# Moving the decay factors of a retention layer to k and to the evacuation, with fronts scheduled further ahead of the channel mixer

## The chip, the cores and the metric

The kernel runs on one core of one Trainium2 chip. The metric is device time in microseconds (us). Times are medians of all executions. Two executions fell into a slower state that has a longer span; the ratios leave them out. A ratio is the mean time of one kernel's fast runs over the mean of the other's fast runs of the same rounds, so it isn't quite the ratio of the medians that stand beside it.

## The reference

Four batches, eight heads, 768 steps, head size 64. First a linear attention with decay, then a mixer over tokens and one over channels (d_tok 256, d_ch 1536):

```python
state = gamma * state + einsum('bhd,bhe->bhde', k[:, :, t], v[:, :, t])
y[:, :, t] = scale * einsum('bhd,bhde->bhe', q[:, :, t], state)
x  = y of all heads side by side                  # [batch, 768, 512]
u  = x + (relu(x^T @ w_tok1) @ w_tok2)^T          # token mixer
out = u + relu(u @ w_ch1) @ w_ch2                 # channel mixer
```

## The kernel before

The recurrence runs in six chunks of 128 steps. The decay inside a chunk is split into two factors that depend on the position alone: one on q, one on v. A **front** is the work on one pair of heads of one batch, attention and token mixer, up to `uT`, the transposed input of the channel mixer; four fronts make a batch. The channel mixer is the **back**. As to the engines: DVE scales q, POOL casts k and scales v, PE does products and transposes, ACT evacuates.

```python
def front(b, p):                                   # eleven steps, a yield after each
    kc = nc.gpsimd.tensor_copy(k16, kf)            # L138 (access patterns cut)
    for j in range(2):                             # one head each
        nc.gpsimd.tensor_scalar(v16[:, :, j, :], vf[...], gv[:, h:h + 1], None, ALU.mult)   # L142
    for j in range(2):
        nc.vector.tensor_scalar(q16[:, :, j, :], qf[...], gq[:, h:h + 1], None, ALU.mult)   # L146
    yield kc
    ...                        # k transposed; k^T v into U (DVE), q transposed, masks (DVE, L192)
    nc.scalar.copy(xo, y)                          # L207, y leaves PSUM
    nc.gpsimd.tensor_copy(x16, xo)                 # L208, f16 for the token mixer
    ...                        # L214, relu, L224 token mixer; L227 add on DVE; L228 cast of u on POOL
    nc.scalar.copy(uT[:, p], tp)                   # L233

for p in range(NP):
    load(0, p)                                     # k, v, q of a pair: three DMAs on one queue (q1)
for s, p, kc in fronts(0):
    if s == 0 and p in (0, 3):
        with tc.issue_after(kc.ins):               # POOL issues the weights (q0) when it gets there
            load_weights(p // 3)
for b in range(B):
    if b + 1 < B:
        ...                                        # loads of b + 1; steps of its fronts
    for us in back(b):                             # spread between the steps of the mixer of b
        ...
```

Every engine works through its own instructions in the order that the build gives it, so an instruction that waits holds all that stand behind it.

## Time and profile before

| | before |
|---|---|
| time, median (lowest to highest) | 251.18 us (250.8 to 251.71) |
| span of the profiled run, granted clock | 249.1 us, 0.984 |
| last uT copy of batch 0 ends | 57.3 us |
| PE idle from there to 245.4 | 13.7 us |
| busy PE / DVE / ACT / POOL | 208.8 / 116.8 / 106.4 / 92.3 us |

```profile
kf<-in_k_dram SPq DMA_DIRECT2D x1, 384.0 KB, 9.0
```

One of six weight transfers goes out at 29.8, and the other five only after 36.9: in between, POOL waits 2.77 us for an add of DVE, casts u (1.13) and scales v (2.46). This k, issued at 29.41, lands 9.0 us later, at 38.4, when the five have hardly begun: from 36 to 40 the weights' queue moves 0.07 MB.

### The profile page before, as it was taken

What the parts mean: (1) busy time and instruction counts of PE and PEld (TensorE: products, weight loads), DVE (VectorE), ACT (ScalarE), POOL (GpSimd) and SP (SyncE); (2) the same over time, 40 slices, a digit from 0 to 9 for tenths busy, and PEclk for the clock granted to TensorE, in tenths of its full rate; (3) what the DMA queues carried; (4) which work ended last, traced back from release to release, by engine and by line L of the source; (5) the groups of instructions that cost most, each with busy time, mean ns of one, the idle gap of its engine ahead of it and who ended that gap; (6) DMA issues with size and microseconds to landing.
All of it is one profiled execution on the core that took longest, in us unless ns stands there. A gap on an engine that the chain in (4) does not pass through costs nothing.

```text
span 249.1 us, 4702 instructions
## 1 busy us (share of the span) xinstructions
PE 208.8 (84%) x1888; PEld 133.6 (54%) x1888; DVE 116.8 (47%) x270; ACT 106.4 (43%) x211; POOL 92.3 (37%) x128
## 2 busy tenths in 40 slices
PE   1448675679989797889798898799899999999994
PEld 0347564456646574456555564466556665554641
DVE  3466447915747445327566445136455354203012
ACT  2233443208804582228615480248435743450710
POOL 4654669943543433621616253520511203100000
PEclk9999999959999999999999999999999999999999
DMA  8999999999949992949862001110011002102112
GB/s 160 228 232 221 204 213 190 196 196 235 214 102 234 228 220 39 216 105 233 153 163 89 0 3 42 42 45 0 3 64 66 0 3 86 45 0 84 42 45 84
DMA packets 82198, 29.41 MB, mean 118 GB/s; under 512 B 75008, under 2 KB 79104, under 8 KB 82176
## 3 DMA queue, kind: packets, MB, share of 16 engines
q1 hardware_dynamic: 77952, 25.17, 49.1%
q0 software_dynamic: 4224, 3.93, 9.6%
q8 instruction: 15, 0.25, 0.4%
q14 instruction: 7, 0.06, 0.1%
HBM read 26.74 MB, written 6.29 MB: 133 GB/s over the span
## 4 chain that ended last, share of the span: by engine, by line
PE 59%; POOL 22%; ACT 7%; DMA 3%; issue 3%; DVE 2%; SPq 2%; POOLq 0%; DVEq 0%; ACTq 0%
PE acc L261 21%; PE acc L253 19%; POOL v L142 14%; PE acc L214 4%; POOL x L208 3%; PE acc L224 3%; DMA vf<-in_v_dram 3%; PE acc L189 3%; ACT h L256 3%; PE tp L232 2%; POOL u L228 2%; SPq L121 2%; PE tp L155 2%; POOL k L138 2%; ACT qT L157 1%
## 5 line engine op out<-in xcount | busy, mean ns | idle before, releaser
L253 PE MATMUL acc<-uT,wc 128*128 128x384 f16 x384 | 74.5, 329 | 0.0
L261 PE MATMUL acc<-wc,h 128*128 128x512 f16 x288 | 71.7, 379 | 0.0
L256 ACT ACTIVATE h<-acc 128x384 f16<-128x384 f32 x96 | 46.7, 498 | 25.0 <-PE acc L253 24.0
L192 DVE TENSOR_TENSOR am<-acc,mask 128x384 f16<-128x384 f32 x64 | 32.8, 551 | 34.4 <-PE acc L189 34.3
L253 PEld LDWEIGHTS <-wc 128*128 128x128 f16 x384 | 34.5, 99 | 18.3 <-issue 0.5
L142 POOL TENSOR_SCALAR v<-vf,gv 128x384 f16<-128x384 f32 x32 | 40.2, 1265 | 8.8 <-DMA vf<-in_v_dram 6.7
L261 PEld LDWEIGHTS <-h 128*128 128x128 f16 x288 | 25.5, 98 | 21.8
L228 POOL CAST u<-x 128x384 f16<-128x384 f32 x32 | 15.8, 510 | 53.0 <-DVE x L227 52.7
L208 POOL CAST x<-x 128x384 f16<-128x384 f32 x32 | 16.5, 518 | 49.3 <-ACT x L207 45.4
L214 PE MATMUL acc<-x,wt 128*128 128x128 f16 x192 | 18.3, 239 | 18.2 <-POOL x L208 18.0
L266 DVE TENSOR_TENSOR o<-x,acc 128x512 f32<-128x512 f32 x24 | 16.5, 686 | 33.5 <-PE acc L261 33.2
L233 ACT COPY uT<-tp 128x768 f16<-128x768 f16 x16 | 12.8, 797 | 41.2 <-PE tp L232 41.2
L214 PEld LDWEIGHTS <-wt 128*128 128x128 f16 x192 | 14.6, 107 | 23.1 <-issue 20.6
L207 ACT COPY x<-acc 128x384 f32<-128x384 f32 x32 | 15.5, 484 | 22.6 <-PE acc L204 22.2
L227 DVE TENSOR_TENSOR x<-x,acc 128x384 f32<-128x384 f32 x32 | 16.6, 550 | 15.9 <-PE acc L224 15.2
L175 DVE SCALAR_TENSOR_TENSOR U<-U,gp,acc 128x128 f32<-128x128 f32 x64 | 22.1, 346 | 2.6
L173 DVE COPY U<-acc 128x128 f32<-128x128 f32 x16 | 4.7, 292 | 35.6 <-PE acc L167 35.6
L146 DVE TENSOR_SCALAR q<-qf,gq 128x384 f16<-128x384 f32 x32 | 18.5, 602 | 5.5 <-DMA qf<-in_q_dram 5.4
L204 PE MATMUL acc<-v,am 128*128 128x64 f16 x192 | 16.7, 205 | 0.7 <-DVE am L192 0.7
L204 PEld LDWEIGHTS <-am 128*128 128x128 f16 x192 | 14.4, 106 | 4.8 <-DVE am L192 0.9
L216 ACT ACTIVATE h<-acc 128x256 f16<-128x256 f32 x16 | 6.1, 380 | 25.4 <-PE acc L214 25.3
L157 ACT COPY qT<-tp 128x768 f16<-128x768 f16 x16 | 12.7, 794 | 9.5 <-PE tp L155 9.5
(40 smaller groups left out, 192.7 us busy)
## 6 DMA issues: line engine op xcount, KB each, us to landing
kf<-in_k_dram SPq DMA_DIRECT2D x16, 384.0 KB, 6.5
vf<-in_v_dram SPq DMA_DIRECT2D x16, 384.0 KB, 6.3
qf<-in_q_dram SPq DMA_DIRECT2D x16, 384.0 KB, 6.5
out_dram<-o SPq DMA_DIRECT2D x24, 256.0 KB, 2.0
wc<-in_moe_w_ch_dram POOLq DMA_DIRECT2D x6, 512.0 KB, 11.4
wt<-in_moe_w_tok_dram POOLq DMA_DIRECT2D x2, 384.0 KB, 7.0
```

The costliest lines, as they stand in the source:

```text
L142: nc.gpsimd.tensor_scalar(v16[:, :, j, :], vf[:, j * NC:(j + 1) * NC, :], gv[:, h:h + 1], None, ALU.mult)
L146: nc.vector.tensor_scalar(q16[:, :, j, :], qf[:, j * NC:(j + 1) * NC, :], gq[:, h:h + 1], None, ALU.mult)
L175: nc.vector.scalar_tensor_tensor(U[:, c], U[:, c - 1], gp[:, p:p + 1], s, ALU.mult, ALU.add)
L192: nc.vector.tensor_tensor(am, a[j][:, :HC], mask, ALU.mult)
L204: nc.tensor.matmul(o[:, j * D:(j + 1) * D], ams[2 * hf + j][:, i], v16[:, c, j], start=(c == 0), stop=(c == 0 or j == 1))
L208: nc.gpsimd.tensor_copy(x16[:, hf * HC:(hf + 1) * HC], xo)
L214: nc.tensor.matmul(acc[:, jt * P:(jt + 1) * P], wt1[:, i, jt * P:(jt + 1) * P], x16[:, i], start=(i == 0), stop=(i == NC - 1))
L227: nc.vector.tensor_tensor(xo, xo, acc[:, :HC * P].rearrange("p (i d) -> p i d", d=P), ALU.add)
L228: nc.gpsimd.tensor_copy(u16[:, hf * HC:(hf + 1) * HC], xo)
L253: nc.tensor.matmul(acc[:, :SH], w[:, ct, (ft % FW) * P:(ft % FW + 1) * P], uT[:, ct, sh * SH:(sh + 1) * SH], start=(ct == 0), stop=(ct == ...
L256: nc.scalar.activation(h2[:, ft], acc[:, :SH], AF.Relu)
L261: nc.tensor.matmul(acc, h2[:, ft, i * P:(i + 1) * P], wc2[ft // FW][:, ft % FW], start=(ft == 0), stop=(ft == NF - 1))
```

## The change

The factors move. One factor now sits on k alone (`gk`), which must be multiplied anyway, and the factor that was on q is applied to the finished y as it leaves PSUM. So q and v need only casts. The schedule is rebuilt too: steps of fronts and mixer are put in a list ordered by an assumed time, with the fronts up to two batches ahead, and the loads of batch 1 are asked for within the fronts of batch 0. The token weights go out with pair 1 in place of pair 0. Buffer counts are cut or raised to fit.

```diff
-        kc = nc.gpsimd.tensor_copy(k16..., kf...)
-            nc.gpsimd.tensor_scalar(v16..., vf..., gv[:, h:h + 1], None, ALU.mult)   # two heads
-            nc.vector.tensor_scalar(q16..., qf..., gq[:, h:h + 1], None, ALU.mult)   # two heads
+            nc.vector.tensor_scalar(k16..., kf..., gk[:, h:h + 1], None, ALU.mult)   # two heads
+        vc = nc.gpsimd.tensor_copy(v16..., vf...)
+        nc.gpsimd.tensor_copy(q16..., qf...)                    # a step later
...
-            nc.scalar.copy(xo, y...)
+            if hf == 0:                                         # ACT, one head at a time
+                nc.scalar.mul(x[...], yv[...], gy[:, h:h + 1])
+            else:                                               # DVE, gyw = gy made wide at setup
+                nc.vector.tensor_tensor(x[...], yv, g.to_broadcast([P, HC, P]), ALU.mult)
...
+        if s == 3:
+            load(1, p, after=ins if p < 3 else None)            # ins: the copy of qT, pair p of batch 0
...
+            f0 = t0 + 10.0 if b == 0 else t0 - LEAD             # LEAD 9, mixer 31, front 16 model units
+            f1 = t0 + PERIOD - LEAD
+            add(fronts(b + 1, 5), [f0 + (f1 - f0) * i / n for i in range(n)], ("front", b + 1))
```

The argument `after` makes a load of batch 1 wait for ACT's copy of qT of the same pair of batch 0, for the first three pairs.

More of the change, by code (lines that the diff above doesn't have):

```diff
@@ L48 @@
     am_p = ctx.enter_context(tc.tile_pool(name="amp", bufs=8))
-    x_p = ctx.enter_context(tc.tile_pool(name="xp", bufs=2))
+    x_p = ctx.enter_context(tc.tile_pool(name="xp", bufs=3))
     mlp_p = ctx.enter_context(tc.tile_pool(name="mlp", bufs=2))
@@ L70 @@
     nc.vector.tensor_scalar(lgs, lgs, itp, None, ALU.mult)
-    gq = const_p.tile([P, H], FP, name="gq")
-    gv = const_p.tile([P, H], FP, name="gv")
-    nc.scalar.activation(gv, lgs, AF.Exp, scale=-1.0)
-    nc.scalar.activation(gq, lgs, AF.Exp, bias=lnsc, scale=1.0)
+    gk = const_p.tile([P, H], FP, name="gk")
+    gy = const_p.tile([P, H], FP, name="gy")
+    nc.scalar.activation(gk, lgs, AF.Exp, scale=-1.0)
+    nc.scalar.activation(gy, lgs, AF.Exp, bias=lnsc, scale=1.0)
     ident16 = const_p.tile([P, P], F16, name="ident16")
@@ L87 @@
     )
+    gyw = const_p.tile([P, H, D], FP, name="gyw")
+    nc.vector.memset(gyw, 1.0)
+    for h in range(H):
+        nc.gpsimd.tensor_scalar(gyw[:, h], gyw[:, h], gy[:, h:h + 1], None, ALU.mult)
     NR = 3
@@ L115, with load @@
     loaded = {}
-    def load(b, p):
+    def load(b, p, after=None):
         got = []
@@ L120, in load @@
             t = load_p.tile([P, 2 * NC, D], FP, name=f"{nm}f")
-            nc.sync.dma_start(
+            dma = nc.sync.dma_start(
                 out=t, in_=src[b, 2 * p:2 * p + 2].rearrange("h (c p) d -> p (h c) d", p=P))
+            if after is not None:
+                tc.add_manual_dep(
+                    dma.ins, after.ins.name,
+                    mybir.DependencyInfo(mybir.DependencyClass.Sync, mybir.DependencyReason.DATA),
+                    reason="the weights come first")
             got.append(t)
@@ L134, in front, with half @@
         kf, vf, qf = loaded.pop((b, p))
-        q16 = att_p.tile([P, NC, 2, D], F16, name="q16")
-        k16 = att_p.tile([P, NC, 2, D], F16, name="k16")
-        v16 = att_p.tile([P, NC, 2, D], F16, name="v16")
-        kc = nc.gpsimd.tensor_copy(k16.rearrange("p c h d -> p h c d"),
-                                   kf.rearrange("p (h c) d -> p h c d", h=2))
+        def half(hf):
+            return slice(hf * HC, (hf + 1) * HC)
+        k16 = att_p.tile([P, NC, 2, D], F16, name="k16", bufs=2)
+        v16 = att_p.tile([P, NC, 2, D], F16, name="v16", bufs=3)
+        q16 = att_p.tile([P, NC, 2, D], F16, name="q16", bufs=2)
         for j in range(2):
             h = 2 * p + j
-            nc.gpsimd.tensor_scalar(v16[:, :, j, :], vf[:, j * NC:(j + 1) * NC, :],
-                                    gv[:, h:h + 1], None, ALU.mult)
-        for j in range(2):
-            h = 2 * p + j
-            nc.vector.tensor_scalar(q16[:, :, j, :], qf[:, j * NC:(j + 1) * NC, :],
-                                    gq[:, h:h + 1], None, ALU.mult)
-        yield kc
-        qT = att_p.tile([P, S], F16, name="qT")
-        kT = att_p.tile([P, S], F16, name="kT")
+            nc.vector.tensor_scalar(k16[:, :, j, :], kf[:, j * NC:(j + 1) * NC, :],
+                                    gk[:, h:h + 1], None, ALU.mult)
+        vc = nc.gpsimd.tensor_copy(v16.rearrange("p c h d -> p h c d"),
+                                   vf.rearrange("p (h c) d -> p h c d", h=2))
+        yield vc
+        qT = att_p.tile([P, S], F16, name="qT", bufs=3)
+        kT = att_p.tile([P, S], F16, name="kT", bufs=3)
         def turn(src, dst):
@@ L156, in turn @@
                                     src[:, c].rearrange("p h d -> p (h d)"), ident16)
-            nc.scalar.copy(dst, tp[:, :S])
+            return nc.scalar.copy(dst, tp[:, :S])
         turn(k16, kT)
+        nc.gpsimd.tensor_copy(q16.rearrange("p c h d -> p h c d"),
+                              qf.rearrange("p (h c) d -> p h c d", h=2))
         yield
-        U = att_p.tile([P, NC - 1, P], FP, name="U")
+        U = att_p.tile([P, NC - 1, P], FP, name="U", bufs=2)
         R = r16[(b * NP + p) % NR]
@@ L179, in front @@
         yield
-        turn(q16, qT)
-        yield
+        turned = turn(q16, qT)
+        yield turned
         ams = []
@@ L194, in front @@
             yield
-        x16 = att_p.tile([P, NC, P], F16, name="x16")
+        x16 = att_p.tile([P, NC, P], F16, name="x16", bufs=2)
         for hf in range(2):
@@ L205, in front @@
                                      start=(c == 0), stop=(c == 0 or j == 1))
-            xo = x[:, hf * HC:(hf + 1) * HC, pc]
-            nc.scalar.copy(xo, y[:, :HC * P].rearrange("p (i d) -> p i d", d=P))
-            nc.gpsimd.tensor_copy(x16[:, hf * HC:(hf + 1) * HC], xo)
+            yv = y[:, :HC * P].rearrange("p (i d) -> p i d", d=P)
+            if hf == 0:
+                for j in range(2):
+                    h = 2 * p + j
+                    nc.scalar.mul(x[:, half(hf), h * D:(h + 1) * D], yv[:, :, j * D:(j + 1) * D],
+                                  gy[:, h:h + 1])
+            else:
+                g = gyw[:, 2 * p:2 * p + 2].rearrange("p (o h) d -> p o (h d)", o=1)
+                nc.vector.tensor_tensor(x[:, half(hf), pc], yv, g.to_broadcast([P, HC, P]), ALU.mult)
+            nc.gpsimd.tensor_copy(x16[:, half(hf)], x[:, half(hf), pc])
             yield
-        h1 = att_p.tile([P, NJ, P], F16, name="h1")
+        h1 = att_p.tile([P, NJ, P], F16, name="h1", bufs=2)
         acc = bank()
@@ L217, in front @@
         yield
-        u16 = att_p.tile([P, NC, P], F16, name="u16")
+        u16 = att_p.tile([P, NC, P], F16, name="u16", bufs=2)
         for hf in range(2):
@@ L225, in front @@
                                      start=(jt == 0), stop=(jt == NJ - 1))
-            xo = x[:, hf * HC:(hf + 1) * HC, pc]
+            xo = x[:, half(hf), pc]
             nc.vector.tensor_tensor(xo, xo, acc[:, :HC * P].rearrange("p (i d) -> p i d", d=P), ALU.add)
-            nc.gpsimd.tensor_copy(u16[:, hf * HC:(hf + 1) * HC], xo)
+            nc.gpsimd.tensor_copy(u16[:, half(hf)], xo)
         yield
@@ L236, with fronts @@
     NS = 11
-    SKEW = 5
-    def fronts(b):
+    def fronts(b, skew):
         gens = [front(b, p) for p in range(NP)]
-        for _, s, p in sorted((SKEW * p + s, s, p) for p in range(NP) for s in range(NS)):
+        for _, s, p in sorted((skew * p + s, s, p) for p in range(NP) for s in range(NS)):
             yield s, p, next(gens[p])
+    BACK_STEPS = 2 * (NF * [0.65] + HC * 3 * [0.86])
     def back(b):
@@ L256, in back @@
                 nc.scalar.activation(h2[:, ft], acc[:, :SH], AF.Relu)
-                yield 0.65
+                yield
             for i in range(HC):
@@ L263, in back @@
                     if ft % 4 == 3 and ft < NF - 1:
-                        yield 0.86
+                        yield
                 o = o_p.tile([P, C], FP, name="o")
@@ L268, in back, with add @@
                 nc.sync.dma_start(out=out[b, t0:t0 + P, :], in_=o)
-                yield 0.86
+                yield
     for p in range(NP):
         load(0, p)
-    for s, p, kc in fronts(0):
-        if s == 0 and p in (0, 3):
-            with tc.issue_after(kc.ins):
+    for s, p, ins in fronts(0, 4):
+        if s == 0 and p in (1, 3):
+            with tc.issue_after(ins.ins):
                 load_weights(p // 3)
-    BACK_US = 31.0
-    for b in range(B):
-        steps = None
-        if b + 1 < B:
-            for p in range(NP):
-                load(b + 1, p)
-            steps = fronts(b + 1)
-        spent, done, total = 0.0, 0, NP * NS
-        for us in back(b):
-            spent += us
-            while steps and done < total and done < spent / BACK_US * total:
-                next(steps)
-                done += 1
-        for _ in steps or ():
-            pass
+        if s == 3:
+            load(1, p, after=ins if p < 3 else None)
+    FRONT_US, BACK_US, LEAD = 16.0, 31.0, 9.0
+    PERIOD = FRONT_US + BACK_US
+    todo = []
+    def add(steps, times, kind):
+        for n, t in enumerate(times):
+            todo.append((t, len(todo), steps, kind))
+    for b in range(B):
+        t0 = b * PERIOD
+        gen = back(b)
+        us = BACK_STEPS
+        span = PERIOD if b + 1 < B else BACK_US
+        run = 0.0
+        times = []
+        for d in us:
+            times.append(t0 + run / BACK_US * span)
+            run += d
+        add(gen, times, ("back", b))
+        if b + 1 < B:
+            f0 = t0 + 10.0 if b == 0 else t0 - LEAD
+            f1 = t0 + PERIOD - LEAD
+            n = NP * NS
+            add(fronts(b + 1, 5), [f0 + (f1 - f0) * i / n for i in range(n)], ("front", b + 1))
+    for t, _, gen, (kind, b) in sorted(todo, key=lambda e: e[:2]):
+        got = next(gen)
+        if kind == "front" and b + 1 < B and got[0] == 3:
+            load(b + 1, got[1])
 _INS = ['q', 'k', 'v', 'moe_w_tok1', 'moe_w_tok2', 'moe_w_ch1', 'moe_w_ch2']
```

## The prediction

> **What bounds the kernel now.** I read the page of the kernel before first: busy shares, the forty slices, the chain that ended last.
>
> ```profile
> PE 208.8 (84%) x1888; PEld 133.6 (54%) x1888; DVE 116.8 (47%) x270; ACT 106.4 (43%) x211; POOL 92.3 (37%) x128
> PE   1448675679989797889798898799899999999994
> DMA  8999999999949992949862001110011002102112
> PE 59%; POOL 22%; ACT 7%; DMA 3%; issue 3%; DVE 2%; SPq 2%; POOLq 0%; DVEq 0%; ACTq 0%
> ```
>
> One slice is 6.2 us. PE is below 8 in most of the first nine slices, mostly 8 or 9 in the middle and full to the end but for the last store, where only the channel mixer of the last batch runs. DMA is full for about 70 us and then nearly idle. POOL, busy for only 37%, carries 22% of the chain. So there are three stages with three limits.
>
> I then cut the span into those stages and took the busy time of each engine:
>
> ```profile
> 0.00:57.00 57.00, 34.11 (x318) 27.47 (x319) 30.62 (x82) 17.43 (x31) 36.27 (x51) 0.94 1.19 205
> 57.00:214.50 157.50, 143.78 (x1407) 90.07 (x1406) 82.08 (x182) 76.75 (x156) 56.00 (x77) 1.00 0.47 101
> 214.50:245.40 30.90, 30.90 (x167) 16.02 (x164) 3.43 (x5) 12.24 (x25) 0.00 (x0) 1.00 0.14 52
> ```
>
> The columns are the stretch, its length, then PE, PEld, DVE, ACT and POOL busy. I put the first cut at 57 because the chain in order of time shows the last uT copy of batch 0 at 56.51; only then can the mixer run unhindered. The middle has 157.5 - 143.8 = **13.7 us of PE idle**; the last stretch has none. After 245.4 there are 3.7 us of final add and store. The run time exceeds the span by about 2 us (251.3 against 249.1).
>
> Next, the groups by line and the waits of PE, to see who stops it:
>
> ```profile
> L142 POOL TENSOR_SCALAR v<-vf,gv 128x384 f16<-128x384 f32 x32 | 40.2, 1265 | 8.8 <-DMA vf<-in_v_dram 6.7
> L208 POOL CAST x<-x 128x384 f16<-128x384 f32 x32 | 16.5, 518 | 49.3 <-ACT x L207 45.4
> L146 DVE TENSOR_SCALAR q<-qf,gq 128x384 f16<-128x384 f32 x32 | 18.5, 602 | 5.5 <-DMA qf<-in_q_dram 5.4
> PE acc L214 <- POOL x L208: 12.8, 9, 1.8
> ```
>
> The last line is the wait list for 54 to 190: nine waits, 12.8 us in all, the longest 1.8. The token mixer's first matmuls (L214) wait for POOL's cast of x, and that explains nearly all of the 13.7 us. The POOL timeline says why the cast is late:
>
> ```profile
> 102.86 0.51 POOL L208 CAST x<-x 128x384 f16<-128x384 f32 x1 [1.98 <-ACT x L207]
> 103.52 2.46 POOL L142 TENSOR_SCALAR v<-vf,gv 128x384 f16<-128x384 f32 x2 [0.15 <-PE acc L204]
> 105.93 0.50 POOL L208 CAST x<-x 128x384 f16<-128x384 f32 x1
> ```
>
> Between the two halves of one pair's x, POOL scales the next pair's v for 2.46 us; L214 starts at 106.48 after an idle of 1.82.
>
> In the start the same instruction rules. The last q of batch 0 is issued at 21.31 and lands some 6.4 us later, at 28, yet the front ends at 57. From 40 to 54 POOL is busy 10.8 of 14 us: v scaling for batch 0 and already for batch 1, casts, and the descriptors of the channel weights.
>
> **What the Trainium skill says.** "GPSIMD Engine Reference", section 4.1, calls POOL about 2x slower than VectorE for two-input work and roughly line rate for one input. The trace agrees only for the cast: the k cast of 768 elements takes 844 ns, 1.1 ns each, while the per-partition scale takes 3.3 ns each (1265 over 384).
>
> "SBUF — State Buffer", "Who interferes with whom": VectorE and GpSimd share a port pair, taken for a whole instruction, and a VectorE tensor_scalar can take it. The trace fits: DVE's q scale takes 404 ns at its shortest and 2400 at its longest, beside POOL's v.
>
> "DMA: Bandwidth & Descriptors", "Queues, rings and completion order": an engine round-robins between queues by packet. From 40 to 44 us the trace agrees (packets, MB, share):
>
> ```profile
> q0 software_dynamic: 613, 0.61, 91.0%
> q1 hardware_dynamic: 616, 0.16, 29.3%
> ```
>
> With equal packet counts the weights move 0.153 MB/us and the loads 0.04, against about 0.22 alone.
>
> "ScalarE: Activation LUTs", "What ACT_TABLE_LOAD costs", gives 186 ns + 0.833 ns an element, and 93 more for a pointer operand. The 384-element copy fits: 506 against 484.
>
> **The change part by part**, per pair of heads (16 pairs).
>
> POOL loses the k cast (0.84) and two v scales (2.53), and gains casts of v and q (0.84 each). With the x and u casts, two halves each, it goes from 5.43 to 3.74 us a pair, 27 us in all. Setup adds eight small scales for gyw: 64 x 3.3 ns plus some 0.1, near 0.3 us each, 2.5 in all, before v lands.
>
> DVE trades the q scale for an equal k scale and gains one evacuation of y, about 0.55 (the mask product of the same shape and source takes 551 ns). That is +8.8 us in all, less any time no longer lost to POOL's lock. Per batch DVE needs about 32 us, in a PE period of about 47.
>
> ACT replaces two copies (0.97) by two scaled copies of 192 elements. The skill's formula gives 186 + 160 + 93 = 439 ns each, so 0.88: nothing to speak of.
>
> PE has the same instructions. From the stage table the steady work and the last mixer are 143.8 + 30.9 = 174.7 us of busy time; with what front 1 did before 57 I take **175.5**.
>
> *The steady stage.* POOL's block between two x casts shrinks from 2.46 to 0.83 (or two of 0.83), a gain of up to 1.63 where the waits were 1.1 to 1.8. So most of the 12.8 us should go. Fronts also run about 9 model units ahead of the mixer, so a late uT no longer stops the next batch. Against it: the second half of y now queues in DVE behind a chain of U updates (1.9 us). I leave **4.5 us** of stalls.
>
> *The start.* The loads follow each other every 1.75 us, the first landing at 4.66: the twelfth at 4.66 + 11 x 1.75 = 23.9. The token weights, 0.79 MB, hold the loads back for about 5 us at a fifth of their rate: 4.2 more, so the last q lands at 28, as now. From there one front needs the q cast 0.83, transposes 0.65, copy 0.8, products 0.5, mask 1.0, y 0.7, evacuation 0.55, x cast 0.5, the two token products 1.3 each, relu 0.4, add 0.55, cast 0.5, transposes 0.65 and copy 0.8. That is 11.0 us, with 2.5 of semaphore steps 13.5 us. POOL also issues six weight transfers at 0.79, right after the v cast of pair 3 and so ahead of its q cast: 4.7 us, most of which I count, 3.5. Front 0 ends at 28 + 13.5 + 3.5 = **45** in place of 57.
>
> Are the weights there? Issued near 28 to 33, 3.15 MB at 0.155 MB/us take 20 us: all landed by about 49. The first half is in by 39, and the second is needed some 10 us after 45. Good. The loads of batch 1 then have about 10 of 12 to go: 49 + 17.5 = 66. The dense fronts of batch 1 want their last pair near 70, the second already near 53: a wait of 1 or 2 us, inside my 4.5.
>
> Sum: 45 + 175.5 + 4.5 + 3.7 = 228.7 of span; with 2 us more about **230 us**, against 251.3.
>
> **The rivals.**
> (a) *The start is bound by DMA, not POOL.* Batches 0 and 1 and all weights are about 25 + 25 + 24 us of transfer, and they keep DMA full to 74 us either way. If the fronts of batch 1 are issued ahead of their loads, PE and DVE, which work in order, stand still on k. The trace has two such waits for v (6.7 us) already. Against it: the mixer of batch 0 offers 31 us of independent PE work. It would cost 5 to 8 us: about 237.
> (b) *The wait moves from POOL to DVE.* y's second half, k, U, mask and the add are then all on one queue, and L214 waits for DVE instead. DVE's 32 of 47 us speaks against a bound, its bursts speak for some waits. If half of the 13 us stay, 233 to 235.
> (c) *POOL's descriptor block in the start.* If it keeps pair 3 back as v does now, front 0 ends at 50: 235.
> (d) *Everything is hidden and PE is the floor.* Front 0 ends at 41, stalls of 1: 221.
> (e) No gain would need both the start and the waits to be rebuilt elsewhere; I see no term that large.
>
> **Range and chances.** The end of front 0 (41 to 51) and the stalls (1 to 9) are the two loose terms, and the rest is PE time that was measured. Together 220 to 240. Within 2% of before means over 246, which needs the start gain gone and half the waits kept: 6%. Slower: 1%.
>
> **What will show it.** PE busy unchanged, near 205 to 209. POOL down to about 65, DVE up to about 125. L214's wait for x near zero. The last uT copy of batch 0 near 45, and PE nearly solid from there. If I am wrong by more than the range, I expect PE waiting on the first transposes of batch 1 (rival a), or L214 waiting behind DVE (rival b). Two things could falsify the sum altogether: the order of the instructions, which the build chooses and I can't see, and a lower PE rate in the denser start: the twelve L224 matmuls took 1.44 us near 52 and 0.67 later.

## More of the kernel before

One more view matters for what came later: when POOL issued the channel weights (start, duration, instruction, count), and how long the second pair of batch 1 took to load when it was issued at 29.41.

```profile
29.80 0.82 POOL L106 DMA_DIRECT2D wc<-in_moe_w_ch_dram  x1
...
34.51 2.46 POOL L142 TENSOR_SCALAR v<-vf,gv 128x384 f16<-128x384 f32 x2
36.93 1.55 POOL L106 DMA_DIRECT2D wc<-in_moe_w_ch_dram  x2
38.46 2.36 POOL L110 DMA_DIRECT2D wc<-in_moe_w_ch_dram  x3
```

## The result, and the profile after

The changed kernel takes **247.87 us** (246.64 to 248.13) against 251.18: a ratio of 0.9855, 95% interval 0.9823 to 0.9888. It is 1.4% faster, within the 2% that I had called the same; I had predicted 8.5%, and the measured time lies outside my range of 220 to 240.

The page of the kernel after: busy time, PE and its granted clock in 40 slices of 6.1 us, and the chain that ended last by engine.

```profile
PE 203.7 (83%) x1888; PEld 129.3 (53%) x1888; DVE 119.8 (49%) x287; ACT 105.1 (43%) x211; POOL 68.7 (28%) x120
PE   0475745016998999999999999999999999999993
PEclk9999985555899999999999999999999999999998
PE 63%; DMA 17%; POOL 8%; issue 6%; ACT 3%; DVE 2%; SPq 0%; POOLq 0%; DVEq 0%; ACTq 0%
```

From the eleventh slice on PE is full: the middle did what I expected. But in the eighth and ninth, where before has 6 and 7, PE stands at 0 and 1, and DMA has gone from 3% to 17% of the chain. By stage (stretch, length, PE, PEld, DVE, ACT, POOL busy, granted clock, DMA share, GB/s):

```profile
40.00:60.00 20.00, 4.09 (x40) 3.34 (x39) 4.00 (x9) 1.31 (x3) 4.29 (x7) 0.50 1.21 210
...
80.00:210.10 130.10, 128.45 (x1276) 80.91 (x1274) 75.79 (x171) 66.34 (x136) 35.97 (x62) 1.00 0.42 95
210.10:241.30 31.20, 31.16 (x169) 16.25 (x166) 4.13 (x6) 11.77 (x24) 0.00 (x0) 1.00 0.14 51
```

Hardly an engine works from 40 to 60, only the DMA does; in the same stretch of the kernel before PE was busy for 15.23 us. The rows by line that answer to L142, L214 and L146 of before (busy, mean ns, idle ahead of them and what ended it) confirm the costs: the v cast takes 851 ns (the q cast 847), and the waits for x are down to 2.0 us at the token mixer (L233). What is new is the k scale's idle time.

```profile
L156 POOL CAST v<-vf 128x768 f16<-128x768 f32 x16 | 13.6, 851 | 15.8 <-DMA vf<-in_v_dram 13.3 <-PE acc L216 2.4
L233 PE MATMUL acc<-x,wt 128*128 128x128 f16 x192 | 16.6, 236 | 4.7 <-DMA wt<-in_moe_w_tok_dram 2.5 <-POOL x L227 2.0
L154 DVE TENSOR_SCALAR k<-kf,gk 128x384 f16<-128x384 f32 x32 | 14.5, 464 | 19.0 <-DMA kf<-in_k_dram 18.9
```

The timeline of DVE shows which k (in brackets the idle time ahead and what ended it):

```profile
35.48 1.39 DVE L154 TENSOR_SCALAR k<-kf,gk 128x384 f16<-128x384 f32 x2
53.10 0.75 DVE L154 TENSOR_SCALAR k<-kf,gk 128x384 f16<-128x384 f32 x2 [16.22 <-DMA kf<-in_k_dram]
53.76 1.94 DVE L204 TENSOR_TENSOR am<-acc,mask 128x384 f16<-128x384 f32 x4
55.62 1.01 DVE L246 TENSOR_TENSOR x<-x,acc 128x384 f32<-128x384 f32 x2
```

The k at 35.48 belongs to pair 0 of **batch 1**, the k at 53.10 to pair 1 of batch 1. Behind it in the same queue stand the masks (L204) of batch 0's last pair and the add (L246) of the pair ahead of it. From 45 to 66, PE's longest wait is put down to exactly those masks (L243 is the second product of the token mixer, here of the pair ahead):

```profile
PE acc L243 <- DVE am L204: 14.3, 1, 14.3
```

Everything of batch 0 stops: its last uT copy starts at 64.16 in place of 56.51. POOL is caught likewise, and the first two lines of its timeline say why the data were late:

```profile
28.55 2.31 POOL L111 DMA_DIRECT2D wc<-in_moe_w_ch_dram  x3
30.84 2.24 POOL L115 DMA_DIRECT2D wc<-in_moe_w_ch_dram  x3
...
44.20 0.83 POOL L170 CAST q<-qf 128x768 f16<-128x768 f32 x1 [7.53 <-DMA qf<-in_q_dram]
54.84 0.83 POOL L156 CAST v<-vf 128x768 f16<-128x768 f32 x1 [9.82 <-DMA vf<-in_v_dram]
```

POOL issues all six weight transfers in one block, by 33.1. (The lighter v isn't the only reason: `schedule_only` below keeps the v scaling and has them out by 34.8.) This k is issued at 30.05, hardly later than the 29.41 of before, but now the weights are in the DMA engines with it. The DMA view from 36 to 40 and the transfer itself (KB, us from issue to landing):

```profile
q0 software_dynamic: 612, 0.61, 89.7%
q1 hardware_dynamic: 611, 0.16, 29.3%
...
kf<-in_k_dram SPq DMA_DIRECT2D x1, 384.0 KB, 23.0
```

Packet for packet the queues are even, so in bytes the loads get 0.16 MB in 4 us, 0.04 MB/us. With the weights gone, from 52 to 56, they move 0.94 MB in 4 us. The k takes 23.0 us in place of 9.0: at 0.04 MB/us its own 384 KB and those still ahead of it need about that.

So the balance of spans is: the start is 7.7 us longer (65.0 against 57.3, each the end of that uT copy), what follows up to the last store is 11.8 shorter (176.3 against 188.1), the tail equal; together 4.1, and the spans differ by 4.2 (249.1 against 244.9; the profile of the changed kernel is of its fastest execution, and the medians differ by 3.3).

### The profile page after: what moved, and what is told of

The parts are those of the page before. It is cut to its first block, busy times and chain, and to the rows that moved or that the text cites. A ratio compares the mean times of both kernels' runs of the same rounds, so it can differ in the third digit from the quotient of the medians.

```text
span 244.9 us, 4710 instructions
## 1 busy us (share of the span) xinstructions
PE 203.7 (83%) x1888; PEld 129.3 (53%) x1888; DVE 119.8 (49%) x287; ACT 105.1 (43%) x211; POOL 68.7 (28%) x120
## 2 busy tenths in 40 slices
DMA packets 82198, 29.41 MB, mean 120 GB/s; under 512 B 75008, under 2 KB 79104, under 8 KB 82176
## 4 chain that ended last, share of the span: by engine, by line
PE 63%; DMA 17%; POOL 8%; issue 6%; ACT 3%; DVE 2%; SPq 0%; POOLq 0%; DVEq 0%; ACTq 0%
PE acc L281 22%; PE acc L273 21%; DMA qf<-in_q_dram 12%; PE acc L233 5%; PE acc L243 3%; DMA wt<-in_moe_w_tok_dram 3%; PE tp L165 3%; PE acc L201 3%; PE tp L251 3%; DMA vf<-in_v_dram 2%; POOL v L156 2%; POOL q L170 2%; POOL x L227 2%; POOL gyw L92 1%; POOL u L247 1%
## 5 line engine op out<-in xcount | busy, mean ns | idle before, releaser
L273 PE MATMUL acc<-uT,wc 128*128 128x384 f16 x384 | 72.8, 327 | 0.0
L204 DVE TENSOR_TENSOR am<-acc,mask 128x384 f16<-128x384 f32 x64 | 32.4, 552 | 14.6 <-PE acc L201 14.2
L286 DVE TENSOR_TENSOR o<-x,acc 128x512 f32<-128x512 f32 x24 | 16.5, 686 | 43.2 <-PE acc L281 42.9
L243 PE MATMUL acc<-h,wt 128*128 128x128 f16 x192 | 15.3, 236 | 15.0 <-DVE am L204 14.3
L154 DVE TENSOR_SCALAR k<-kf,gk 128x384 f16<-128x384 f32 x32 | 14.5, 464 | 19.0 <-DMA kf<-in_k_dram 18.9
L243 PEld LDWEIGHTS <-wt 128*128 128x128 f16 x192 | 13.5, 106 | 18.1 <-issue 15.9
L246 DVE TENSOR_TENSOR x<-x,acc 128x384 f32<-128x384 f32 x32 | 16.4, 550 | 13.1 <-PE acc L243 12.6
L222 ACT ACTIVATE x<-acc,gy 128x192 f32<-128x192 f32 x32 | 11.8, 429 | 21.8 <-PE acc L216 21.8
L233 PE MATMUL acc<-x,wt 128*128 128x128 f16 x192 | 16.6, 236 | 4.7 <-DMA wt<-in_moe_w_tok_dram 2.5
L170 POOL CAST q<-qf 128x768 f16<-128x768 f32 x16 | 13.6, 847 | 23.3 <-DMA qf<-in_q_dram 8.5
L233 PEld LDWEIGHTS <-wt 128*128 128x128 f16 x192 | 13.9, 106 | 8.9 <-issue 3.9
L156 POOL CAST v<-vf 128x768 f16<-128x768 f32 x16 | 13.6, 851 | 15.8 <-DMA vf<-in_v_dram 13.3
L167 ACT COPY kT<-tp 128x768 f16<-128x768 f16 x16 | 12.8, 802 | 11.7 <-PE tp L165 11.7
```

The costliest lines, as they stand in the source:

```text
L156: vc = nc.gpsimd.tensor_copy(v16.rearrange("p c h d -> p h c d"), vf.rearrange("p (h c) d -> p h c d", h=2))
L167: return nc.scalar.copy(dst, tp[:, :S])
L170: nc.gpsimd.tensor_copy(q16.rearrange("p c h d -> p h c d"), qf.rearrange("p (h c) d -> p h c d", h=2))
L204: nc.vector.tensor_tensor(am, a[j][:, :HC], mask, ALU.mult)
L233: nc.tensor.matmul(acc[:, jt * P:(jt + 1) * P], wt1[:, i, jt * P:(jt + 1) * P], x16[:, i], start=(i == 0), stop=(i == NC - 1))
L243: nc.tensor.matmul(acc[:, i * P:(i + 1) * P], wt2[:, jt, t], h1[:, jt], start=(jt == 0), stop=(jt == NJ - 1))
```

## The experiments

My theory after the comparison: **two in-order queues, DVE and POOL, carry conversions of batch 1 ahead of the last work of batch 0, and those conversions wait for loads that share the DMA engines with the weights.** Rivals: one queue alone is to blame; the loads are late for another reason (the explicit dependency); fronts start too early; or one half of the change, scaling or schedule, does the harm and the other the good. Fourteen kernels were run. The column "PE 40–80" is PE's busy time between 40 and 80 us, a measure of how open the start is.

| run | time, us | ratio to before | last uT copy of batch 0 starts | PE 40–80 |
|---|---|---|---|---|
| before | 251.18 | | 56.51 | 33.82 |
| after | 247.87 | 0.9855 | 64.16 | 22.60 |
| order_dve, order_pool (one run each) | 247.13, 247.45 | | 64.61, 64.60 | 22.46, 22.90 |
| order_both | 237.06 | 0.9431 | 47.72 | 33.44 |
| late_weights | 244.81 | 0.9743 | 47.07 | 28.39 |
| late_weights_order (one run) | 244.05 | | 48.58 | 27.95 |
| third_weights (one run, wrong result) | 229.99 | | 48.05 | 37.64 |
| no_load_dep (one run) | 247.61 | | 65.15 | 22.89 |
| scaling_only | 245.9 | 0.9792 | 64.11 | 24.45 |
| schedule_only | 258.94 | 1.0312 | 65.99 | 23.05 |
| later_front (one run) | 251.34 | | 64.53 | 23.21 |
| order_later | 237.92 | 0.9448 | 47.38 | 34.59 |
| scaling_order | 241.9 | 0.9649 | 50.47 | 30.63 |
| order_mid | 234.21 | 0.9329 | 47.39 | 36.24 |
| order_mid_split | 238.29 | 0.95 | 47.30 | 32.99 |

### Order on one queue, and on both

The edit makes batch 1's conversions follow batch 0's last add (DVE) or last u cast (POOL), by edges for the build's ordering that add no wait. `order_dve` has the first line, `order_pool` the other two, `order_both` all. In the traces four k scales on DVE and two v and two q casts on POOL change place; in `order_both` PE, ACT and the load queue keep their order to the instruction.

```diff
+            if b == 1: behind(ks, "dve")      # k scale
+        if b == 1: behind(vc, "pool")         # v cast
+        if b == 1: behind(qc, "pool")         # q cast
```

> Edit: the DVE half of the ordering alone (k of batch 1 behind batch 0's last add); POOL keeps the order of the changed kernel. Theory A: POOL still stands on q and v of batch 1, until q of pair 1 lands near 56, ahead of the u and x casts of batch 0's pairs 2 and 3, so the last uT copy stays at 63-65 us and the time within 2 us of 247.9. If DVE alone were the blocker, the gain would be nearly that of both, 15 us or more.

> Edit: the POOL half alone (v and q of batch 1 behind batch 0's last u cast); DVE keeps the order of the changed kernel. Theory A: DVE still stands on k of batch 1, pair 1, until 53, ahead of the masks of pair 3 and the adds of pair 2, so the last uT copy comes at 61-64 us, a gain of 1-4 us. If POOL alone were the blocker (rival C too), the gain would be 10 us or more.

> Edit: edges without a wait put the conversions of batch 1 (k on DVE; v and q on POOL) behind the last DVE add and the last POOL cast of batch 0's front. In the built program only pairs 0 and 1 of batch 1 move, by a few places on DVE and POOL; PE, ACT and SP keep their order to the instruction. Theory A (head of the line): in the changed kernel DVE stood 16.2 us on k of batch 1, pair 1, whose load took 23.0 us to land beside the channel weights, and POOL stood 7.5 and 9.8 us on the like, while the masks and casts of batch 0's pairs 2 and 3 were ready behind them. Then the last uT copy of batch 0 falls from 65 us to 45-47, and the time from 247.9 to 228-231 us. Rival B (the start is bound by DMA bandwidth whatever the order): the last uT copy stays at 60 or later, and the time at 244-248. Rival C (POOL's block of six weight transfers of 4.6 us holds pair 3 back): at most 1-2 us of change.

Each half gave nothing: 247.13 and 247.45, with the last uT copy of batch 0 still near 64.6 (for `order_pool` I had expected 61 to 64). Both together gave 237.06 (ratio 0.9431, interval 0.9404 to 0.9459). Either queue alone holds batch 0, and the position of these eight instructions is worth 10.8 us (medians of different rounds). The last uT copy of batch 0 in `order_both`, and the timeline of its DVE:

```profile
47.72 0.80 ACT L267 COPY uT<-tp 128x768 f16<-128x768 f16 x1 [2.80 <-PE tp L266]
```
```profile
46.50 0.99 DVE L161 TENSOR_SCALAR k<-kf,gk 128x384 f16<-128x384 f32 x2
53.93 0.75 DVE L161 TENSOR_SCALAR k<-kf,gk 128x384 f16<-128x384 f32 x2 [6.44 <-DMA kf<-in_k_dram]
```

The same k now costs DVE 6.4 us instead of 16.2, and it no longer stands ahead of batch 0. The time misses my expected 228 to 231: the loads are as late as before, and batch 1's fronts meet them between 50 and 64 (DVE waits another 3.41 us for the next k, at 58.71). That remainder is what the next runs are about.

### The weights: issued later, or only a third of them

`late_weights` leaves the order and puts the six transfers on POOL behind the q cast of batch 1's pair 1.

```diff
+        if (b, p) == (1, 1):
+            for d in wdmas: ...   # each weight DMA ordered behind this q cast
```

> Edit: the order of batch 1's conversions stays ahead of batch 0's last work, as in the changed kernel, but POOL issues the six channel-weight transfers behind its casts of batch 1, pair 1, near 40 us and not at 28.5. Theory A says that the early conversions hurt only because the weights starve their loads: with the loads undisturbed, k, v and q of batch 1's pairs 0 and 1 land by about 39 us, DVE has no wait over 3 us there, and the last uT copy of batch 0 is at 45-50. The mixer then waits for weights, and starts in earnest near 53-57: 236-241 us. Rival B (bandwidth whatever the order): the same bytes move in the same time, so no gain, 246-250.

The loads issued between 28 and 32 now land after 6.1 to 6.6 us (the k: 6.3, against 23.0), DVE has no wait for k between 25 and 60, and the last uT copy starts at 47.07. So it is the weights that made the loads late. But POOL reached the weights only at 47.5, and the channel mixer now waits for them, as the list of PE's waits from 45 to 90 shows (us in total, times, longest):

```profile
PE acc L281 <- DMA wc<-in_moe_w_ch_dram: 4.9, 1, 4.9
PE acc L289 <- DMA wc<-in_moe_w_ch_dram: 3.7, 2, 2.0
```

I had taken too little for that: 244.81, not 236 to 241.

`third_weights` loads one third of each weight and uses it three times, a wrong result, with 1.05 MB on the queue in place of 3.15.

```diff
-            for i in range(NW):
+            for i in range(1):        # both weights
-                w = wc1[ft // FW]
+                w = wc1[0]            # wc2 likewise
```

> The changed kernel with one of the three parts of each channel weight loaded and used three times (a wrong result on purpose): 1.05 MB of weights in place of 3.15, everything else alike. My theory (loads of batch 1 starved by the weights' queue): the k of pair 1 of batch 1 lands by about 42 in place of 53, last uT copy of batch 0 near 48 without any order imposed, and the time 230 to 236 us. Rival (the loads are late for another reason, or the conversions ahead of batch 0 hold it back even when their data are there): last uT copy after 55 and 240 us or more.

It ran in 229.99 us, with the last uT copy at 48.05: without two thirds of the weights' traffic the whole change is worth what I had predicted. (POOL also issues two weight transfers in place of six, so the run isn't clean of that.)

One reading of these two runs isn't allowed. With other weight traffic the build itself had chosen another order: in both, the k of pair 1 of batch 1 stands *behind* the last masks of batch 0. So they show that the weights delay the loads, but not that an early conversion does no harm when its data are there. `late_weights_order` settles that. It issues the weights behind batch 0's last u cast and holds the order of the changed kernel by edges, at the two places where it had hurt.

```diff
+    # DVE: masks of batch 0 pair 3 and adds of pair 2 behind the k scale of (1, 1)
+    # POOL: u casts of pair 2 and x casts of pair 3 behind the q cast of (1, 1)
+    # POOL: the six weight transfers behind the last u cast of batch 0
```

> The channel weights issued late (behind batch 0's last u cast), with the order of the changed kernel held by edges: the k of pairs 0 and 1 of batch 1 ahead of the last masks of batch 0 on DVE, the v and q of both ahead of the last u and x casts on POOL. In the two runs with less or later weight traffic the build had moved those conversions back by itself, so neither told whether the order does harm when the data are there. My theory (order does harm only with late loads): the loads land some 6.5 us after their issue, k of pair 1 by 37, q of pair 1 by 41; the last uT copy of batch 0 starts at 48 to 51 in place of 64. The time says little, since the mixer waits for weights issued near 50: 244 to 251 us. Rival (the order alone holds batch 0): the last uT copy after 56.

The timeline of its DVE has four k scales, pairs 0 and 1 of batch 1, right ahead of the masks, as in the changed kernel, and without a wait:

```profile
35.77 1.81 DVE L158 TENSOR_SCALAR k<-kf,gk 128x384 f16<-128x384 f32 x4
37.50 1.94 DVE L215 TENSOR_TENSOR am<-acc,mask 128x384 f16<-128x384 f32 x4
```

The last uT copy starts at 48.58 in place of 64.16, in the window I had named. So neither the order nor the late loads holds the front alone: order with loads on time 48.6, late loads with the order mended 47.7, the two together 64.2. (Its time, 244.05, suffers from the late weights like that of `late_weights`.)

### The explicit dependency

```diff
-            load(1, p, after=ins if p < 3 else None)
+            load(1, p)
```

> The changed kernel without the explicit dependency that puts the first three pairs' loads of batch 1 behind the channel weights' issue; every engine keeps the same order of instructions. My theory (two in-order queues that hold batch 0 behind conversions of batch 1 whose loads share the DMA engines with the weights): the dependency is satisfied before those loads could be issued anyway, since the load queue itself reaches them near 30 us, so no change: 247 to 249 us, last uT copy of batch 0 near 64. Rival (the dependency itself makes the loads late): the k of pair 1 of batch 1 lands some 3 us or more earlier, and the time falls to 244 or below.

247.61, every engine's order unchanged, and the last uT copy at 65.15. The dependency is innocent. (My expectation describes it wrongly: the loads waited for the copies of qT, not for the weights' issue. The edit takes away all that was there.)

### The two halves of the change

`scaling_only` is the kernel before with the factors moved; `schedule_only` is the kernel after with the old scaling (POOL casts k and scales v, DVE scales q, ACT copies y).

> Edit: the kernel before with the new scaling alone (k on DVE, v and q cast on POOL, outputs scaled as they leave PSUM); loads, weights and schedule as before. Theory: the middle gains by itself, POOL near 69 us busy and PE's wait for x after 57 us under 4 us in place of 12.8. The start does not: POOL, relieved of v, issues the channel weights some 8 us sooner, they starve batch 1's loads, and its conversions stand ahead of batch 0's: last uT copy at 60-66 us against 56.5. Together 243-249. If the loss in the start came from the new schedule and not from the scaling, the start would stay near 57 or better and the time fall to 238-241.

> Edit: the changed kernel with the scaling of before (k cast and v scaled on POOL, q scaled on DVE, outputs only copied); the new schedule, load order and three x buffers stay. Theory: POOL is at 92 us again and its 2.5 us of v still stand between two x casts, so PE's waits for x in the middle come back, 6-13 us; the start is no better than in the changed kernel, last uT copy 62-70. Together 250-258. If the running ahead of the fronts were what removed the waits, the middle would be as clean as in the changed kernel (under 3 us) and the time 246-250.

Scaling alone: 245.9 (ratio 0.9792, interval 0.9718 to 0.9865), faster, but unclear whether by 2%. Schedule alone: 258.94 (1.0312, interval 1.0269 to 1.0355), slower than before and just above my 250 to 258. The waits of PE after the start tell the halves apart; first `scaling_only` from 64 us on, then `schedule_only` from 66 on (us in total, times, longest; in the latter L224 is the token mixer's first product and L218 the x cast):

```profile
PE acc L191 <- ACT qT L157: 1.0, 1, 1.0
PE acc L224 <- POOL x L218: 0.4, 1, 0.4
```
```profile
PE acc L224 <- POOL x L218: 14.2, 10, 2.1
```

The scaling removes the waits for x; the schedule, with POOL still slow, keeps them (14.2 us, where I had expected 6 to 13). The profile of `schedule_only` is of the slow state, so I take from it only that these waits are there. The start is late in both, near 64 and 66. In both POOL has issued all weights by 36.2 at the latest, against 40.8 in the kernel before, and conversions of batch 1 then wait for their loads (7.7 us at most in `scaling_only`, 14.7 in `schedule_only`). Each half has the last weights out earlier, so the loss isn't owed to one of them.

### Fronts of batch 1 later, or spread

`later_front` starts batch 1's fronts 8 model units later; `order_later` does so on top of `order_both`; `order_mid` starts them 4 later and ends them 6 later on top of `order_both`.

```diff
-            f0 = t0 + 10.0 if b == 0 else t0 - LEAD
+            f0 = t0 + 18.0 if b == 0 else t0 - LEAD            # order_mid: 14.0
-            f1 = t0 + PERIOD - LEAD
+            f1 = t0 + PERIOD - (3.0 if b == 0 else LEAD)       # order_mid only
```

> Edit: batch 1's fronts 18 units late as in the run beside it, but without the ordering edges, so DVE and POOL still have the conversions of batch 1's pairs 0 and 1 ahead of batch 0's last masks and casts. Theory A: the start stays blocked, last uT copy at 63-66 us, and the later fronts alone give at most 2 us: 245-249. If the early conversions did not matter, this would do as well as the run with the edges, under 238.

> Edit: the ordering of both engines as before, and the first front steps of batch 1 are laid 18 model units after the start of the mixer in place of 10. In the ordering run the last uT copy came at 47.7, but then DVE stood on k of batch 1, pair 2, for 6.4 and 3.4 us (loads land every 1.75 us and only from 51 on), PE waited 5.4 us in all, and its matmuls ran at half the rate for some us after it. Theory A with loads (batch 1's fronts come before their loads): with mixer work alone until about 60 us, PE's waits between 48 and 90 fall under 1.5 us, and the time from 237 to 228-232. Rival (the loss of those 8 us is in the mixer or in ACT, not in the loads): 235-238, no change.

> The changed kernel with batch 1's conversions behind batch 0 on both queues, and its fronts spread over more of batch 0's mixer (start 4 model units later, end 6 later). My theory: with the start unblocked (last uT copy near 48) what is left is the wait for the third pair of batch 1 between 56 and 72 and the dense fronts after it; spreading them should take some of the 6 to 8 us of idle there: 231 to 236 us. Rival (the idle comes from the late loads whatever the spread): the same as with the order alone, 236 to 239.

Alone the later start doesn't help: 251.34, above my 245 to 249, and batch 0's last uT copy is at 64.53, since the build still puts those conversions ahead. With the order freed it gave 237.92, no better than `order_both` and a miss of my 228 to 232: squeezed into less time, the fronts of batch 1 left gaps in PE after 64 (busy for 20.69 of the 26 us to 90, against 23.30 in `order_both`). Spread over more of the mixer, `order_mid` gave **234.21** (ratio 0.9329, interval 0.929 to 0.9369), the best correct kernel and faster than both given ones. Its worst stretch is still the one where the loads are late (columns as in the stage table above):

```profile
56.00:64.00 8.00, 5.96 (x53) 3.51 (x51) 4.67 (x13) 2.07 (x3) 2.98 (x4) 0.91 1.03 205
```

`order_mid_split` asks whether that can be had too: the three transfers of the second weight go behind batch 0's last u cast.

```diff
+                for d in wdmas: behind(d, "pool")     # here: the second weight's three
```

> The variant with the order and the spread fronts (234.2 us), with only the first weight issued early and the three transfers of the second behind batch 0's last u cast, near 46: 1.57 MB beside the loads from 28 on in place of 3.15. My theory (the weights' share of the engines sets what is left in the start): the k of pair 1 of batch 1 lands near 43 in place of 53, the idle of PE between 56 and 64 falls, and the second weight is there by about 58, just when the mixer's second product wants it: 229 to 233 us. Rival (the starvation is only moved to the loads after 46, or the mixer waits for the second weight): 234 us or more.

238.29 (ratio 0.95, interval 0.9463 to 0.9537), on the rival's side. POOL issues the second weight at 46.81, and the list of PE's waits from 45 to 200 has it first:

```profile
PE acc L299 <- DMA wc<-in_moe_w_ch_dram: 5.3, 3, 2.4
```

The loads suffer again too: from 52 to 56 they move 0.19 MB beside 0.55 MB of weights. With the weights early the loads beside them are late; with some or all of them late the mixer waits. I found no better place for them among those that I tried.

### The old schedule with the new scaling and the order

`scaling_order` is `scaling_only` with the edges of `order_both`.

> The kernel before with the scaling half of the change and the same order on both queues, but the old schedule of fronts. My theory (the block in the start is one of order, the waits in the middle are removed by the scaling alone, the schedule adds little): last uT copy of batch 0 near 48, 230 to 237 us, within 2 per cent of the whole change with the order. Rival (the new schedule is what pays once the start is free): 240 us or more here.

241.9 (ratio 0.9649): on the rival's side of my threshold. So the new schedule does pay once the start is open: by ratio 0.9431 against 0.9649, some 2%. It pays in the start as well: from 80 to 210 PE is busy 128.66 us here and 128.17 in `order_both`, but from 56 to 64 only 1.95 against 5.06. There DVE waits 6.17 us for a k of batch 1 here, and PE's mixer instructions stand among steps of batch 1 that need it.

## Why the prediction was wrong

**The step that failed: "Front 0 ends at 28 + 13.5 + 3.5 = 45 in place of 57."** It ended at 65.0. The sum held POOL's descriptors and the chain of batch 0's own instructions and had no term for instructions of batch 1 standing in the same queues. `order_both` measures the parts: with those out of the way the front ends at 48.5 (47.72 and 0.80 for the copy). So 16.5 of the 20.0 us are the block, and 3.5 are chain and descriptors that I took too short. Of those 3.5, 1.8 are there by the q cast of the last pair, which I had at 31.5 and which starts at 33.27, when POOL has issued the weights; the rest comes after it. (I had also read the landing of the last q wrongly: 7.4 us after its issue in the kernel before, not 6.4, and 9.0 after the change. It doesn't decide, as POOL is at the weights until 33.1.)

**The step beside it: "a wait of 1 or 2 us, inside my 4.5" for the loads of batch 1.** I had the starved rate right (0.04 MB/us, from the trace) and applied it to the wrong question: I asked when the mixer's PE work would want those loads, not which instructions would be queued behind them. The k waited for at DVE cost 16.2 us at once.

**Rival (a) had the mechanism and lost its size to one sentence.** I wrote that DVE and PE, working in order, would stand still on k, and then: "the mixer of batch 0 offers 31 us of independent PE work. It would cost 5 to 8 us: about 237." The mixer can't start until batch 0's fronts are done, and the conversions stood ahead of those. Where they don't, as in `order_both`, the rival's number is what was measured: 237.06. Its size is partly luck: of the 7.6 us by which that span exceeds my 228.7, 3.5 are the later end of front 0, 2.6 are PE idle beyond my 4.5 (7.1 from 48.5 to 232.7), and 1.6 are PE's busy time. Where the loads are starved less, as in `third_weights` (the k lands after 11.8 us in place of 23.0), it is my central number: 229.99 against 230, a span of 228.3 against 228.7. That agreement is partly luck, as its front 0 ends at 48.9 and not at 45, and less was lost after it than I had set aside.

**The steady stage was right.** The waits for x went, by the scaling alone, as argued. In the whole change PE is idle 2.6 us from 65 to 241.3 (149.0 − 146.39 in the middle and 27.3 − 27.26 at the end), against my 4.5; busy time and stalls together are 176.3 against 180.0. The tail is 3.6 against 3.7. So the predicted span of 228.7 misses by +20.0 − 3.7 − 0.1 = 16.2, which is the 244.9 found.

**The costs by instruction were mostly right.** POOL is busy 68.7 against about 65, DVE 119.8 against up to 125, PE 203.7 against 205 to 209. The scaled copy on ACT takes 429 ns where the formula of "ScalarE: Activation LUTs", "What ACT_TABLE_LOAD costs", gave an estimate of 439. DVE's k scale takes 464 ns on average against 602 for the q scale of the same shape before, a share that I had not sized. It fits the lock that the prediction cites; no run isolates it. The eight small scales for gyw take 472 ns each, not some 300.

**Rivals (b), (c), (d):** y's second half on DVE held POOL's x casts for 2.8 us in all, but the list of PE's waits after 65 us names DVE nowhere, so (b) isn't seen; the descriptor block of (c) is 4.5 us long and counted; (d) fell with front 0, though PE is the bound from 65 us on.

**The clock was low in the start; that it sets the two kernels apart isn't shown.** I had named a lower PE rate as a danger. From 40 to 60 the granted clock is 0.50, and twelve L243 matmuls took 1.44 us at 60.98, as against 0.84 at 30.59. "TensorE: Matmul & The Clock Gate", Part 1, says that after an idle window of about 3.4 us the array falls to half rate until it has been busy as long. The trace agrees only in part: the clock is 0.50 all through the wait of 14.3 us, but it was so from 36 us on already, when PE had had no wait over 2.07 us in the ten us before. `order_both` has the same drop (0.56 from 35.4 to 41.3). And in the kernel before, the same twelve matmuls (there L224) took 1.44 us in all four pairs of batch 0, at 21.58 to 52.36, three times at a recorded clock of 0.99 or 1.00. So durations and recorded clock don't always go together in these traces, and how much of the 3.5 us a lower rate makes isn't separated; the chain of the prediction had taken 1.3 us for each of the two token products. (The prediction's "0.67 later" is from the view of the chain; the timeline, from which the 1.44 can be read, has 0.83.)

I also named "the order of the instructions, which the build chooses and I can't see" as what could falsify the sum, and gave it no width: a chance of 0.07 for everything outside "faster" was too small for a stage whose order I could not read.

**What stays open:** how to have the weights early and the loads not late with a correct result. Of the 4.2 us between `order_mid` and my 230 some 2 are idle time of PE from 56 to 64. `order_later` has only 0.4 there, but loses 5.3 from 64 to 90, where `order_mid` loses 1.1. The rest I have not placed. Loads on a second queue were not tried. Nor were the ordering edges on the unchanged kernel before, which itself had conversions of batch 1 ahead of batch 0's last casts; so how much of the gain of `order_mid` a mended old kernel would have isn't known.

## What to carry to other kernels

When the work of an engine that also issues transfers is made cheaper or put in another order, those transfers can start sooner: look up what will then share the DMA engines, and what in another in-order queue stands behind the data that become late. Before a lead of one batch over another is counted as a gain, check for each engine whether any instruction of the later batch is placed ahead of the earlier batch's last ones, and whether its data will be there; a wait is harmless only if nothing needed stands behind it. If both queues are blocked, undoing one shows nothing, so test them together, and look in each variant's timeline whether the build kept the order that you meant to compare.

## What the Trainium skill lacked or had wrong

- "DMA: Bandwidth & Descriptors", "Queues, rings and completion order": the round robin by packet agrees with the trace (612 against 611 packets in 4 us, if the trace counts what the page calls a packet, which no run shows), but the page gives 9 to 17 descriptors as a typical packet and doesn't say what equal turns mean for unequal packets. Here the loads' packets carried about 0.26 KB and the weights' 1.0 KB, so the loads fell from 0.235 to 0.04 MB/us, and one transfer of 384 KB took 23.0 us in place of 9.0.
- "GPSIMD Engine Reference", section 4.1: "roughly line rate" for one input covers the cast (851 ns for 768 elements) but not the multiplication by a value per partition: 1265 ns for 384 elements and 472 ns for 64, thus an estimate of 2.5 ns an element on top of some 0.3 us (worked out from these two, of which the first writes f16 and the second f32).
- "SBUF — State Buffer", "Who interferes with whom": the lock is described, a size for a mix like this one isn't. A DVE scale of the same shape took 602 ns on average (median 492) beside POOL's v scaling and 464 (median 415) where POOL only casts; that the lock makes this difference isn't shown.
- No page that I read says how far ahead the build may move an instruction of a later stage on an in-order engine, or how to hold it back; an ordering edge without a wait was worth 10.8 us here (247.87 to 237.06, medians of different rounds).
